# Attention and gated feed-forward on one core: a twelve-step pipeline over four tiles, packed row sums, a token-major output projection and queries transposed by DMA

## The chip, the cores and the metric

The kernel runs on one core of a Trainium2 chip. The metric is the device time of one execution in microseconds (us), taken as the median of several executions.

Engine names in the profile: PE is TensorE's matmuls, PEld its weight loads, DVE is VectorE, ACT is ScalarE, POOL is GpSimd, SP is SyncE. "L221" is line 221 of the kernel whose profile is shown. A "bank" is one of the eight 128 x 512 fp32 buffers in PSUM that both kernels allot for PE's results. An "eviction" is the copy of a full bank out of PSUM by ACT or DVE.

## The reference, cut to what matters

```python
# B=4, N=12288 queries per batch, C=128; kv: 384 x 32 positions per batch; d_ff=1536
kv_pool = kv.reshape(B, H//4, 4, W//4, 4, C).mean(axis=(2, 4))   # 768 pooled keys per batch
k = v = kv_pool.reshape(B, -1, C) @ w_sr
s = (q @ k.transpose(0, 2, 1)) / sqrt(C)
a = exp(s - s.max(-1)) ; a /= a.sum(-1) + 1e-9
x = a @ v                                       # attention output, 49152 tokens x 128
out = (relu(x @ w_gate) * (x @ w_val)) @ w_out  # fp32, 49152 x 128
```

Both kernels leave the normalisation to the end: relu and the product are homogeneous, so dividing x by the row sum r divides the output by r squared. They need r (one number per token) only at the output.

## The kernel before

It takes 512 tokens at a time ("a tile", 96 in all). Per tile it computes six score chunks, exp on ACT, six value chunks, row sums, twelve value and twelve gate projections, the output projection, and a turn of the output to token-major. The loop staggers the stages by one tile:

```python
def stage_r(k):                       # row sums: 1 weight column, 6 x 512 columns
    r_ps = psum.tile([1, TSUP], FP32, tag="bank")
    for jc in range(NJC):
        nc.tensor.matmul(r_ps, ones_a, aT[:, jc, :], ...)
    nc.scalar.copy(r_row, r_ps)
...
def stage_moe2(k):                    # output projection, feature-major
    for fb in range(NFB):
        nc.tensor.matmul(oT_ps, wo16[:, fb, :], hT[:, fb, :], ...)   # 12 x 512 columns
    nc.vector.tensor_copy(oT, oT_ps)
def stage_out(k):                     # back to token-major on PE
    for s in range(NSUB):
        nc.tensor.matmul(o_ps[:, s, :], oT[:, s*128:(s+1)*128], ident, is_transpose=True, ...)
    # four tensor_scalar by 1/r^2, then the store
...
for k in range(NTOT + 2):
    stage_qk(k, jcg(0)); stage_out(k - 2)
    stage_moe1(k - 1, [0]); stage_moe1(k - 1, [1])     # value and gate projections
    ...                                                # the rest interleaved; stage_tq: PE transposes
    stage_r(k); stage_rcol(k - 1); stage_moe2(k - 1); stage_load(k + 2)
```

Queries are loaded as fp32 and transposed on PE (`stage_tq`, four fp32 transposes per tile and one DVE copy). The pooled keys are summed by sixteen accumulating DMA transfers per batch on POOL's queue.

The softmax here doesn't subtract the row's maximum and nothing guards it: scores larger than these inputs give would overflow.

Of the kernel before, what the change touches and what calls it, by code (L numbers as in the profile page):

```python
# [9 lines left out]
FP32 = mybir.dt.float32  # L10
# [6 lines left out]
def kernel(  # L17
# [9 lines left out]
):  # L27
    nc = tc.nc
# [4 lines left out]
    HP, WP = H // r, W // r  # L33
    J = HP * WP
    D_FF = moe_w_gate.shape[1]
    NFB = D_FF // 128
    TSUP = 512
    NSUB = TSUP // 128
    NST = N // TSUP
    NJC = J // 128  # L40
    ALPHA = 1.0 / float(J)
    qk_scale = 1.0 / math.sqrt(C)

    assert N % TSUP == 0 and J % 128 == 0 and C == 128 and D_FF % 128 == 0
    assert NFB == 12 and NJC % 2 == 0
    assert J == 128 * NJC

    NTOT = B * NST

    cpool = ctx.enter_context(tc.tile_pool(name="const", bufs=1))  # L50
    wpool = ctx.enter_context(tc.tile_pool(name="wts", bufs=1))
    kvpool = ctx.enter_context(tc.tile_pool(name="kvp", bufs=1))
    spool = ctx.enter_context(tc.tile_pool(name="work", bufs=2))
    psum = ctx.enter_context(tc.tile_pool(name="psum", bufs=8, space=bass.MemoryType.PSUM))

    ident = cpool.tile([128, 128], FP32)
    make_identity(nc, ident)
    ones_a = cpool.tile([128, 1], FP16)
    nc.gpsimd.memset(ones_a, ALPHA)

    w_sr_f32 = wpool.tile([128, C], FP32)
    nc.sync.dma_start(w_sr_f32, w_sr)
    wg16 = wpool.tile([128, D_FF], FP16)
    wv16 = wpool.tile([128, D_FF], FP16)
    wo16 = wpool.tile([128, NFB, 128], FP16)
    for w16, src in (
        (wg16, moe_w_gate),
        (wv16, moe_w_val),
        (wo16, moe_w_out.rearrange("(fb f) c -> f fb c", f=128)),
    ):  # L70
        wstage = kvpool.tile([128, D_FF], FP32, tag="wstage")
        nc.sync.dma_start(wstage, src)
        nc.vector.tensor_copy(w16.rearrange("p ... -> p (...)"), wstage)

    kT_all = wpool.tile([128, B, NJC, 128], FP16)
    v_all = wpool.tile([128, B, NJC, 128], FP16)

    kv_tiles = {}

    def prep_dma(b):  # L80
        parts = []
        for dh in range(r):
            kvp = kvpool.tile([128, NJC, C], FP32, tag=f"kvp{dh}")
            first = True
            for dw in range(r):
                nc.gpsimd.dma_start(  # L86
                    kvp, kv[b][dh::r, dw::r, :],
                    accum_op=(ALU.bypass if first else ALU.add),
                )
                first = False  # L90
            parts.append(kvp)
        kv_tiles[b] = parts

    def prep_compute(b):
        parts = kv_tiles.pop(b)
        kvpT = kvpool.tile([128, NJC, C], FP32, tag="kvpT")
        for jc in range(NJC):
            tp_ps = psum.tile([128, 128], FP32, tag="bank")
            for dh in range(r):
                nc.tensor.matmul(  # L100
                    tp_ps, parts[dh][:, jc, :], ident, is_transpose=True,
                    start=(dh == 0), stop=(dh == r - 1),
                )
            nc.scalar.copy(kvpT[:, jc, :], tp_ps)
        for jc in range(NJC):
            kT_ps = psum.tile([128, 128], FP32, tag="bank")
            nc.tensor.matmul(kT_ps, w_sr_f32, kvpT[:, jc, :], start=True, stop=True)
            nc.scalar.mul(kT_all[:, b, jc, :], kT_ps, qk_scale / (r * r))  # L108
            v_ps = psum.tile([128, 128], FP32, tag="bank")
            nc.tensor.matmul(v_ps, kvpT[:, jc, :], w_sr_f32, start=True, stop=True)  # L110
            nc.scalar.mul(v_all[:, b, jc, :], v_ps, 1.0 / (r * r))

    prep_dma_at = {max(0, b * NST - 6): b for b in range(1, B)}
    prep_compute_at = {max(0, b * NST - 2): b for b in range(1, B)}

    qT_tiles = {}
    aT_tiles = {}
    xT_tiles = {}
    inv2_tiles = {}
    hT_tiles = {}  # L120
    val_tiles = {}
    rrow_tiles = {}
    qraw_tiles = {}

    def glob_tok(k):
        b = k // NST
        st = k % NST
        return b, b * N + st * TSUP, st * TSUP

    def stage_load(k):  # L130
        if not (0 <= k < NTOT):
            return
        b, _, n0 = glob_tok(k)
        q_raw = spool.tile([128, NSUB, C], FP32, tag="q_raw", bufs=4)
        nc.sync.dma_start(
            q_raw, q[b, n0 : n0 + TSUP, :].rearrange("(s p) c -> p s c", p=128)
        )
        qraw_tiles[k] = q_raw

    def stage_tq(k):  # L140
        if not (0 <= k < NTOT):
            return
        q_raw = qraw_tiles.pop(k)
        qT_ps = psum.tile([128, TSUP], FP32, tag="bank")
        for s in range(NSUB):
            nc.tensor.matmul(  # L146
                qT_ps[:, s * 128 : (s + 1) * 128], q_raw[:, s, :], ident,
                is_transpose=True, start=(s == 0), stop=(s == NSUB - 1),
            )
        qT = spool.tile([128, TSUP], FP16, tag="qT", bufs=3)  # L150
        nc.vector.tensor_copy(qT, qT_ps)  # L151
        qT_tiles[k] = qT

    def stage_qk(k, jc_list):
        if not (0 <= k < NTOT) or not jc_list:
            return
        b, _, _ = glob_tok(k)
        if jc_list[0] == 0:
            qT = qT_tiles[k]
            aT = spool.tile([128, NJC, TSUP], FP16, tag="aT", bufs=2)  # L160
            aT_tiles[k] = aT
        else:
            qT = qT_tiles[k]
            aT = aT_tiles[k]
        if jc_list[-1] == NJC - 1:
            qT_tiles.pop(k)
        for jc in jc_list:
            sT_ps = psum.tile([128, TSUP], FP32, tag="bank")
            nc.tensor.matmul(  # L169
                sT_ps, kT_all[:, b, jc, :], qT,  # L170
                start=True, stop=True,
            )
            nc.scalar.activation(aT[:, jc, :], sT_ps, AF.Exp)  # L173

    xtps_tiles = {}

    def stage_av(k, jc_list):
        if not (0 <= k < NTOT) or not jc_list:
            return
        b, _, _ = glob_tok(k)  # L180
        aT = aT_tiles[k]
        if jc_list[0] == 0:
            xt_ps = psum.tile([128, TSUP], FP32, tag="bank")
            xtps_tiles[k] = xt_ps
        else:
            xt_ps = xtps_tiles[k]
        for jc in jc_list:
            nc.tensor.matmul(  # L188
                xt_ps, v_all[:, b, jc, :], aT[:, jc, :],
                start=(jc == 0), stop=(jc == NJC - 1),  # L190
            )
        if jc_list[-1] == NJC - 1:
            xtps_tiles.pop(k)
            xT = spool.tile([128, TSUP], FP16, tag="xT", bufs=3)
            nc.vector.tensor_copy(xT, xt_ps)
            xT_tiles[k] = xT

    def stage_r(k):
        if not (0 <= k < NTOT):
            return  # L200
        aT = aT_tiles.pop(k)
        r_ps = psum.tile([1, TSUP], FP32, tag="bank")
        for jc in range(NJC):
            nc.tensor.matmul(  # L204
                r_ps, ones_a, aT[:, jc, :],
                start=(jc == 0), stop=(jc == NJC - 1),
            )
        r_row = spool.tile([1, TSUP], FP32, tag="r_row", bufs=2)
        nc.scalar.copy(r_row, r_ps)  # L209
        rrow_tiles[k] = r_row  # L210

    def stage_rcol(k):
        if not (0 <= k < NTOT):
            return
        r_row = rrow_tiles.pop(k)
        rcol_ps = psum.tile([128, NSUB], FP32, tag="bank")
        for s in range(NSUB):
            nc.tensor.matmul(  # L218
                rcol_ps[:, s : s + 1], r_row[0:1, s * 128 : (s + 1) * 128],
                ident[0:1, 0:1], is_transpose=True,  # L220
                start=(s == 0), stop=(s == NSUB - 1),  # L221
            )
        rinv = spool.tile([128, NSUB], FP32, tag="rinv", bufs=3)
        nc.vector.reciprocal(rinv, rcol_ps)
        tmp = spool.tile([128, NSUB], FP32, tag="rtmp", bufs=3)
        nc.vector.tensor_scalar(tmp, rinv, ALPHA, None, op0=ALU.mult)
        inv2 = spool.tile([128, NSUB], FP32, tag="inv2", bufs=4)
        nc.vector.tensor_tensor(inv2, tmp, tmp, op=ALU.mult)
        inv2_tiles[k] = inv2

    def stage_moe1(k, fb_list):
        if not (0 <= k < NTOT) or not fb_list:
            return
        if fb_list[0] == 0:
            hT = spool.tile([128, NFB, TSUP], FP16, tag="hT", bufs=2)
            val_sb = spool.tile([128, NFB, TSUP], FP16, tag="val_sb", bufs=2)
# [131 lines left out]
```

## Time and profile before

| | before |
|---|---|
| median of 3 runs | 1434.69 us (1434.51 to 1435.2) |
| profiled span | 1432.5 us |
| first loop matmul | about 61 us |
| one tile in the loop | 14.06 us |

The prediction below shows the totals, the timeline and the waits. Three groups of the page are worth adding, because the change rewrites them. Columns: line, engine, operation, output <- inputs, shape, count | busy us, mean ns of one | idle us of the engine just before, and what ended most of it.

```profile
L276 DVE COPY oT<-oT_ps 128x512 f32<-128x512 f32 x96 | 66.4, 692 | 173.4 <-PE oT_ps L271 173.4
L287 PE MATMUL o_ps<-ident,oT 128*128 128x128 f32 x384 | 62.8, 286 | 33.9 <-DVE oT L276 33.9
L204 PE MATMUL r_ps<-aT,ones_a 128*1 128x512 f16 x576 | 140.1, 378 | 0.0
```

The first two rows are one chain: DVE idles until the last output matmul, copies, and PE idles until the copy is there. The third row is 576 matmuls that use one of PE's 128 columns. Their "mean ns of one" (378) is the length of a pipelined matmul, not its cost; the cost is the distance between starts, 216 ns.

### The profile page before, as it was taken

How to read it: one execution, taken by the hardware profiler on the slowest of the kernel's cores; microseconds unless marked ns; L12 is line 12 of the kernel's file. 1: busy time of each engine (PE TensorE's matmuls, PEld its weight loads, DVE VectorE, ACT ScalarE, POOL GpSimd, SP SyncE). 2: the span in 40 equal slices, each digit the busy share in tenths (PEclk: the TensorE clock that was granted, in tenths of full speed). 3: DMA queues.
4: the chain of work that ended last, by engine and by line, in shares of the span. 5: the costliest groups of instructions: out<-in, count | busy, mean ns of one | idle time of the engine just before them, and what ended most of it. 6: DMA issues, size and time to landing. Idle time of an engine off the chain costs nothing.

```text
span 1432.5 us, 18941 instructions
## 1 busy us (share of the span) xinstructions
PE 1333.7 (93%) x6528; PEld 612.5 (43%) x6528; DVE 1039.6 (73%) x2115; ACT 947.7 (66%) x1897; POOL 81.7 (6%) x71
## 2 busy tenths in 40 slices
PE   0599999999999999999999999999999999999998
PEld 0344444444544444444454444444454444444443
DVE  0177777878677778787768787877767878777776
ACT  0367676767676767676667676766776766667674
POOL 5510000000220000000041000000000000000000
PEclk9999999999999999999999999999999999999999
DMA  9951111111591111111194111111111111111000
GB/s 229 179 93 38 37 45 30 45 30 45 101 148 32 45 30 44 32 43 37 38 169 81 30 45 35 40 37 37 39 36 31 45 37 38 37 37 40 28 23 23
DMA packets 142880, 79.14 MB, mean 55 GB/s; under 512 B 4160, under 2 KB 140992, under 8 KB 142784
## 3 DMA queue, kind: packets, MB, share of 16 engines
q1 hardware_dynamic: 103360, 52.77, 13.0%
q0 software_dynamic: 39424, 25.17, 12.0%
q8 instruction: 51, 0.84, 0.2%
q14 instruction: 45, 0.37, 0.1%
HBM read 52.76 MB, written 25.17 MB: 54 GB/s over the span
## 4 chain that ended last, share of the span: by engine, by line
PE 69%; ACT 21%; DVE 5%; DMA 3%; issue 1%; POOL 1%; DVEq 0%; POOLq 0%
PE oT_ps L271 18%; ACT val_sb L252 14%; PE g_ps L254 12%; PE va_ps L248 10%; PE r_ps L204 9%; PE xt_ps L188 9%; ACT aT L173 7%; DVE oT L276 5%; PE o_ps L287 4%; PE qT_ps L146 3%; DMA kvp<-in_kv_dram 3%; PE rcol_ps L218 2%; PE tp_ps L100 1%; POOL kvp L86 1%; ACT kT_all L108 0%
## 5 line engine op out<-in xcount | busy, mean ns | idle before, releaser
L258 DVE SCALAR_TENSOR_TENSOR hT<-g_ps,val_sb 128x512 f16<-128x512 f32 x1152 | 721.4, 682 | 48.0 <-PE va_ps L248 45.0
L252 ACT CAST val_sb<-va_ps 128x512 f16<-128x512 f32 x1152 | 611.4, 639 | 73.0 <-PE va_ps L248 73.0
L173 ACT ACTIVATE aT<-sT_ps 128x512 f16<-128x512 f32 x576 | 320.9, 625 | 239.1 <-PE sT_ps L169 239.1
L254 PE MATMUL g_ps<-xT,wg 128*128 128x512 f16 x1152 | 436.1, 379 | 9.7
L248 PE MATMUL va_ps<-xT,wv 128*128 128x512 f16 x1152 | 436.6, 379 | 0.1
L271 PE MATMUL oT_ps<-hT,wo 128*128 128x512 f16 x1152 | 265.3, 380 | 0.0
L276 DVE COPY oT<-oT_ps 128x512 f32<-128x512 f32 x96 | 66.4, 692 | 173.4 <-PE oT_ps L271 173.4
L169 PE MATMUL sT_ps<-qT,kT_all 128*128 128x512 f16 x576 | 171.0, 379 | 0.8 <-DVE qT L151 0.8
L293 DVE TENSOR_SCALAR o_sb<-o_ps,inv 128x128 f32<-128x128 f32 x384 | 108.1, 344 | 86.3 <-PE o_ps L287 86.3
L254 PEld LDWEIGHTS <-wg 128*128 128x128 f16 x1152 | 112.7, 98 | 116.8 <-issue 2.4
L248 PEld LDWEIGHTS <-wv 128*128 128x128 f16 x1152 | 112.6, 98 | 114.5 <-issue 1.3
L188 PE MATMUL xt_ps<-aT,v_all 128*128 128x512 f16 x576 | 155.9, 378 | 0.0
L271 PEld LDWEIGHTS <-wo 128*128 128x128 f16 x1152 | 104.8, 98 | 114.8
L204 PE MATMUL r_ps<-aT,ones_a 128*1 128x512 f16 x576 | 140.1, 378 | 0.0
L209 ACT COPY r_row<-r_ps 1x512 f32<-1x512 f32 x96 | 55.2, 575 | 98.3 <-PE r_ps L204 97.0
L86 POOL DMA_DIRECT2D kvp<-in_kv_dram x64 | 80.9, 1379 | 685.1 <-PE tp_ps L100 588.1
L151 DVE CAST qT<-qT_ps 128x512 f16<-128x512 f32 x96 | 66.4, 692 | 55.6 <-PE qT_ps L146 51.7
L287 PE MATMUL o_ps<-ident,oT 128*128 128x128 f32 x384 | 62.8, 286 | 33.9 <-DVE oT L276 33.9
L188 PEld LDWEIGHTS <-v_all 128*128 128x128 f16 x576 | 55.7, 97 | 77.0 <-issue 20.6
L169 PEld LDWEIGHTS <-kT_all 128*128 128x128 f16 x576 | 56.2, 98 | 68.6 <-DVE qT L151 1.0
L204 PEld LDWEIGHTS <-ones_a 128*1 128x1 f16 x576 | 40.2, 82 | 91.8 <-issue 41.3
L287 PEld LDWEIGHTS o_ps<-ident,oT 128*128 128x128 f32 x384 | 40.5, 140 | 80.2 <-DVE oT L276 76.9
(28 smaller groups left out, 374.9 us busy)
## 6 DMA issues: line engine op xcount, KB each, us to landing
kvp<-in_kv_dram POOLq DMA_DIRECT2D x64, 384.0 KB, 6.6
q_raw<-in_q_dram SPq DMA_DIRECT2D x96, 256.0 KB, 2.8
out_dram<-o_sb SPq DMA_DIRECT2D x96, 256.0 KB, 2.3
wstage<-in_moe_w_gate_dram SPq DMA_DIRECT2D x1, 768.0 KB, 4.5
wstage<-in_moe_w_val_dram SPq DMA_DIRECT2D x1, 768.0 KB, 5.8
wstage<-in_moe_w_out_dram SPq DMA_DIRECT2D x1, 768.0 KB, 6.4
w_sr_f<-in_w_sr_dram SPq DMA_DIRECT2D x1, 64.0 KB, 1.7
```

Of the source, the lines that this page charges most:

```text
L169: nc.tensor.matmul(sT_ps, kT_all[:, b, jc, :], qT, start=True, stop=True,)
L173: nc.scalar.activation(aT[:, jc, :], sT_ps, AF.Exp)
L188: nc.tensor.matmul(xt_ps, v_all[:, b, jc, :], aT[:, jc, :], start=(jc == 0), stop=(jc == NJC - 1),)
L204: nc.tensor.matmul(r_ps, ones_a, aT[:, jc, :], start=(jc == 0), stop=(jc == NJC - 1),)
L248: nc.tensor.matmul(va_ps, wv16[:, fb * 128 : (fb + 1) * 128], xT, start=True, stop=True,)
L252: nc.scalar.copy(val_sb[:, fb, :], va_ps)
L254: nc.tensor.matmul(g_ps, wg16[:, fb * 128 : (fb + 1) * 128], xT, start=True, stop=True,)
L258: nc.vector.scalar_tensor_tensor(hT[:, fb, :], g_ps, 0.0, val_sb[:, fb, :], op0=ALU.max, op1=ALU.mult,)
L271: nc.tensor.matmul(oT_ps, wo16[:, fb, :], hT[:, fb, :], start=(fb == 0), stop=(fb == NFB - 1),)
L276: nc.vector.tensor_copy(oT, oT_ps)
L287: nc.tensor.matmul(o_ps[:, s, :], oT[:, s * 128 : (s + 1) * 128], ident, is_transpose=True, start=(s == 0), stop=(s == NSUB - 1),)
L293: nc.vector.tensor_scalar(o_sb[:, s, :], o_ps[:, s, :], inv2[:, s : s + 1], None, op0=ALU.mult,)
```

## The change

Its intent: let PE never wait for the engine it has just fed, and take from PE what another unit can do or what uses it badly.

```diff
-    q_raw fp32; 4 PE transposes + DVE copy per tile
+    nc.gpsimd.dma_start(q16, q[...])                    # fp32 -> fp16 in the transfer, 4 tiles at once
+    nc.sync.dma_start_transpose(qT, q16...)             # 24 in all
-    nc.tensor.matmul(r_ps, ones_a, aT[:, jc, :])        # per tile, [1, 512]
+    for jc in range(NJC):                               # once per 4 tiles
+        for i in range(GRP):
+            nc.tensor.matmul(r_ps[32*i : 32*i+32, :], ones, aTs[g*GRP+i][:, jc, :])   # ones [128, 32]
-    nc.tensor.matmul(oT_ps, wo16[:, fb, :], hT[:, fb, :])              # 12 x 512, copy, 4 transposes
+    for s in range(NS):                                                # 48 x 128, token-major at once
+        nc.tensor.matmul(o_ps[:, s, :], hTs[k][:, fb, s*128:(s+1)*128], wo16[:, fb, :])
-    for k in range(NTOT + 2): stages of tile k, k-1, k-2 ...
+    for k in range(LAG, last + 1):                      # LAG = 3
+        for step in range(NFB):                         # twelve equal steps
+            out_proj(k - LAG - 1, step)
+            value_proj(k - LAG, step)
+            scores(k, step//2)  or  values(k - 1, step//2)
+            gate_proj(k - LAG, step)
+            # row sums in step 2, their transposes in step 5 of every fourth tile
-    kv pooled by accumulating DMA
+    kv loaded plainly (kv_in, 3 buffers, sync and ACT queues), added on DVE;
+    later batches loaded by the sync queue, added on POOL, projected inside the loop
```

The six key chunks of the first batch and the scores and values of the first four tiles run ahead of the loop.

## The prediction

> **What bounds the kernel now.** I read the busy totals first, then the chain of work that ended last, then sixteen microseconds of the timeline in mid-kernel, then the list of waits.
>
> ```profile
> PE 1333.7 (93%) x6528; PEld 612.5 (43%) x6528; DVE 1039.6 (73%) x2115; ACT 947.7 (66%) x1897; POOL 81.7 (6%) x71
> PE 69%; ACT 21%; DVE 5%; DMA 3%; issue 1%; POOL 1%; DVEq 0%; POOLq 0%
> ```
>
> TensorE (PE) is at work for 93% of the span and holds 69% of the chain; no other engine passes 73%. Matmuls overlap, so 93% isn't yet proof. The timeline of one loop turn gives the real paces (start, length, group, count):
>
> ```profile
> 700.34 0.40 PE L218 MATMUL rcol_ps<-ident,r_row 1*128 1x1 f32 x4
> ...
> 700.67 2.76 PE L271 MATMUL oT_ps<-hT,wo 128*128 128x512 f16 x12
> ...
> 704.22 0.66 PE L287 MATMUL o_ps<-ident,oT 128*128 128x128 f32 x4 [0.35 <-DVE oT L276]
> ...
> 708.97 3.12 ACT L252 CAST val_sb<-va_ps 128x512 f16<-128x512 f32 x6
> ...
> 709.75 3.67 DVE L258 SCALAR_TENSOR_TENSOR hT<-g_ps,val_sb 128x512 f16<-128x512 f32 x6
> ...
> 713.01 1.46 PE L204 MATMUL r_ps<-aT,ones_a 128*1 128x512 f16 x6
> ...
> 714.40 0.40 PE L218 MATMUL rcol_ps<-ident,r_row 1*128 1x1 f32 x4
> ```
>
> The same group returns after 714.40-700.34 = **14.06 us**: one 512-token tile. Twelve 512-column matmuls take 2.76 us, one alone 0.38, so the pace is (2.76-0.38)/11 = **0.216 us**. The row sums (one weight column) keep the same pace: (1.46-0.38)/5 = 0.216. Four fp32 transposes run at (0.66-0.286)/3 = 0.125 (0.11 where the queue is full). ScalarE (ACT) evicts one bank per 3.12/6 = **0.52**, VectorE (DVE) one per 3.67/6 = **0.61**.
>
> A tile has 54 matmuls of 512 columns (6 scores, 6 values, 6 row sums, 12 value, 12 gate, 12 output): 54 x 0.216 = 11.66. Eight fp32 transposes (queries, output) add 0.95, four row-sum transposes (0.40-0.20)/3 = 0.067 each, 0.27. Sum 12.9 of 14.06; the remaining 1.2 us is PE waiting. The waits say where (total us, times, longest):
>
> ```profile
> PEld o_ps L287 <- DVE oT L276: 76.9, 91, 0.8
> PEld qT_ps L146 <- DVE hT L258: 57.8, 94, 0.6
> PEld rcol_ps L218 <- issue: 41.6, 95, 0.4
> PEld L204 <- issue: 41.3, 98, 0.6
> ```
>
> Some 0.8, 0.6, 0.4 and 0.4 us per tile on the weight loader (part of each is covered by matmuls in flight): output projection, copy, transpose one after another; a transpose waiting for a bank; and two waits for nothing, each where the row sums begin or end.
>
> The start is the other piece, in the chain in order of time:
>
> ```profile
> 47.46 6.71 DMA kvp<-in_kv_dram
> 54.22 1.54 PE tp_ps L100 x6
> 61.05 1.47 PE sT_ps L169 x6
> ```
>
> Nothing useful runs on PE until 61 us: sixteen accumulating transfers come one by one. 61 + 96 x 14.06 + the tail is the 1432.5 us span.
>
> **What the Trainium skill says.** (1) "TensorE: Matmul & The Clock Gate", section "Back-to-back issue gap", gives about 56 ns as the isolated gap of a 128-column matmul but about 81 ns for a sustained stream of load-and-multiply pairs, and 131 ns for N=512. The trace disagrees with the last (0.216), so I trust the 81 only in part. (2) The same page, "Measured speedup vs the span model": three 32-column strips at once ran 2.38 times as fast as one after another. No strip runs beside another in the kernel before. (3) "TensorEngine Tiling (Array Packing)", section "Key Properties": changing the tiling mode drains the array. The two 0.4 us "issue" waits around the row sums agree with a drain. (4) "Advanced Engine Details and Errata", section "X-Bar Transpose (TRN2)", expects DMA transposes at 350-400 GB/s; no row before shows one.
>
> **The change, part by part**, per tile on PE:
>
> - Scores, values, value and gate projection stay: 36 x 0.216 = **7.78**.
> - Output projection is turned: hT becomes the stationary operand, so 12 matmuls of 512 columns (2.59) become 48 of 128 columns, each with its own weight load, and oT, its copy, four fp32 transposes and four small DVE scalings go. Columns are equal; the open term is the pair's pace. 512 columns in 0.216 scales to 0.054 plus overhead. Loads of 128x128 fp16 weights last 98 ns in the record, against 140 for fp32 and 82 for one column, so filling 128 fp16 columns seems to cost about 16 ns and should hide. I take 0.060: 48 x 0.060 = **2.88**. At 0.081 it would be 3.89.
> - Row sums of four tiles go to four 32-partition strips of one bank. If four stream at once: 6 x 0.216 = 1.30, plus two drains of 0.1, per four tiles: **0.38** per tile instead of 1.30. The row turns into a column by four fp32 transposes per four tiles: 4 x 0.11/4 = **0.11** instead of 0.27.
> - Query transposes leave PE (about 0.45) for 24 DMA transposes of 512 KB, and their DVE copy goes.
> - Sum: 7.78+2.88+0.38+0.11 = **11.15 us**.
>
> ACT has 12+6 evictions: 18 x 0.52 = 9.4; its row copy is gone. DVE has 12 products and one xT copy at 0.61, one output scaling of a whole bank at about 0.7 (estimated from the 0.69 copies) and a quarter of a row-sum copy and two small operations (0.24): 8.9 us. Both lie beside PE, so PE stays the bound, with less spare than the totals before suggest.
>
> The three-tile lag removes the chains: what PE multiplies in a step was made a step, or a tile, earlier. I keep **3%** of waits, because eight banks, two held for a whole tile by open sums, leave six in rotation with ACT at 84% and DVE at 80% of PE's period.
>
> The start: the keys now load plainly on two queues, are pooled on DVE, and four tiles of scores and values run while they arrive. 6.3 MB at the 203 GB/s which the kernel before moved in its first 72 us is 31 us; with queries and latency about 45 us until the loop, of which PE's 10 us of scores are part of the tile sums: 38 net. Pooling of later batches goes to POOL, idle so far, with slack of two tiles. Their 12 projections cost PE about 0.5 us each: 6. The tail: 6.
>
> Total: 96 x 11.15 = 1070; x 0.03 = 32; 38 + 6 + 6 = 50. **1152 us**, ratio 0.80.
>
> **Rivals.**
>
> A. The 128-column pairs are weight-bound. For: 81 ns in the skill, and over half of PE's matmuls come to be of this kind. Against: fp16 loads are short. It adds 48 x 0.021 x 96 = 97 us: about 1250.
>
> B. The strips don't run together (each strip's load waits for the multiply before). For: the drains. Against: the skill's 2.38. Row sums stay at 1.3 per tile: +0.92 x 96 = 88 us, about 1240.
>
> C. Evictions become the bound: DVE's end-of-tile burst (output scaling 0.7, xT 0.6) lets banks run out, so PE stalls about 1 us per tile: 1152 + 96 - 32, about 1215. It would show as PE waiting on DVE or ACT at value and gate projections.
>
> D. In-order queues. The built order puts 60 key loads into the sync queue ahead of the first output store, each fourth waiting for POOL to free a buffer; transposes wait there too. A slow POOL would hold back stores, then DVE and PE, early on: +20 to 40 us once. The DMA transposes are hidden anyway: one per 45 us, 1.5 us at the skill's rate; even ten times slower they fit.
>
> **Range and chances.** The floor is 0.056 per pair, no waits, a quick start: about 1100. One rival in part gives 1200-1240; two in full 1330, still under the 1406 which 2% needs. So 1105 to 1235; faster 0.95, same 0.03, slower 0.02.
>
> **What would show it.** Right: a four-tile period of 44.6-46 us; 48 output matmuls per tile at 0.056-0.065 spacing; row sums 24 in about 1.5 us; PE over 95% busy and no single wait above some 30 us in total; first loop matmul near 45 us. Wrong: spacing near 0.08 (A); row sums taking 5 us per group (B); PE waits on DVE or ACT near 1 us per tile (C); a hole of tens of us before the first stores (D). The prediction fails as a whole only if a DMA transpose takes over 45 us, or POOL starves the later batches.

## The result, and the profile after

| | before | after |
|---|---|---|
| median | 1434.6 us (4 runs) | 1127.94 us (4 runs, 1127.68 to 1128.06) |
| ratio | 1 | 0.7862, 95% interval 0.7851 to 0.7873 |
| profiled span | 1432.5 | 1125.7 |
| one tile in the loop | 14.06 | 43.75/4 = 10.94 |

The totals and the chain of the changed kernel, from its page:

```profile
PE 1077.6 (96%) x8874; PEld 636.3 (57%) x8874; DVE 920.1 (82%) x1470; ACT 909.2 (81%) x1741; POOL 119.8 (11%) x124
PE 94%; DMA 3%; ACT 1%; SPq 1%; DVE 0%; issue 0%; ACTq 0%; DVEq 0%; POOLq 0%
```

PE's share of the chain went from 69% to 94% and ACT's from 21% to 1%: the chain now runs from one matmul to the next. DVE and ACT carry more per unit of time than before and still aren't on it.

One and a half steps and a row-sum group in the timeline (start, length, group, count; other engines and the other matmuls of the steps are left out):

```profile
561.41 0.39 PE L221 MATMUL bank_ps<-wo,hT 128*128 128x128 f16 x4
...
562.28 0.39 PE L221 MATMUL bank_ps<-wo,hT 128*128 128x128 f16 x4
...
562.93 0.38 PE L207 MATMUL bank_ps<-xT,wg 128*128 128x512 f16 x1
563.24 0.98 PEld L170 LDWEIGHTS <-ones 128*32 128x32 f16 x24 [0.42 <-issue]
563.24 1.48 PE L170 MATMUL bank_ps<-aT,ones 128*32 128x512 f16 x24
...
564.65 0.40 PE L221 MATMUL bank_ps<-wo,hT 128*128 128x128 f16 x4
```

A step is 562.28 - 561.41 = 0.87 us: three 512-column matmuls at 0.216 and four 128-column ones at 0.056. That is what PE needs and nothing more. The 24 row-sum matmuls of four tiles start within 1.10 us; with the switch of PE to 32-column strips and back (0.31 us from the matmul before, 0.31 to the one after, where 0.216 is usual) they cost 564.65 - 562.93 - 0.216 = 1.50 us. Before, one tile's six cost 1.48 by the same count.

The waits of the changed kernel (total us, times, longest):

```profile
ACT val L200 <- PE bank_ps L196: 164.6, 568, 2.5
DVE hT L210 <- ACT val L200: 83.2, 312, 0.3
ACT L131 <- DMA parts<-in_kv_dram: 36.1, 1, 36.1
PE bank_ps L133 <- ACT kvT L131: 24.0, 2, 23.6
PE bank_ps L156 <- DVE o_sb L229: 2.1, 1, 2.1
```

ACT waits for PE and DVE for ACT, which is as it should be. Of the two waits of PE, one is at the start and one near 112 us. The start of the changed kernel, from the timeline:

```profile
0.74 35.30 ACTq L101 DMA_DIRECT2D parts<-in_kv_dram  x12
...
16.34 8.27 SPq L84 DMA_TRANSPOSE qT<-q  x1
...
36.07 1.28 ACT L131 ACT_TABLE_LOAD   x1 [36.07 <-DMA parts<-in_kv_dram]
```

ACT issues twelve key loads, and with three buffers the later ones wait until a buffer is free: its first work of its own comes at 36 us. Only then can PE project a key chunk (37.68 us); six chunks follow, some 3.9 us each, and the loop's first matmul is at 61.55 us, no earlier than before.

### The profile page after: what moved, and what is told of

The parts are those of the page before. It is cut to its first block, busy times and chain, and to the rows that moved or that the text cites. A ratio compares the mean times of both kernels' runs of the same rounds, so it can differ in the third digit from the quotient of the medians.

```text
span 1125.7 us, 23319 instructions
## 1 busy us (share of the span) xinstructions
PE 1077.6 (96%) x8874; PEld 636.3 (57%) x8874; DVE 920.1 (82%) x1470; ACT 909.2 (81%) x1741; POOL 119.8 (11%) x124
## 4 chain that ended last, share of the span: by engine, by line
PE 94%; DMA 3%; ACT 1%; SPq 1%; DVE 0%; issue 0%; ACTq 0%; DVEq 0%; POOLq 0%
PE bank_ps L221 23%; PE bank_ps L196 22%; PE bank_ps L207 22%; PE bank_ps L150 11%; PE bank_ps L156 11%; PE bank_ps L170 3%; DMA q<-in_q_dram 1%; PE bank_ps L133 1%; PE bank_ps L182 1%; DMA parts<-in_kv_dram 1%; SPq L84 1%; DMA out_dram<-o_sb 1%; ACT aT L151 1%; PE bank_ps L134 1%; PE bank_ps L126 0%
## 5 line engine op out<-in xcount | busy, mean ns | idle before, releaser
L210 DVE SCALAR_TENSOR_TENSOR hT<-bank_ps,val 128x512 f16<-128x512 f32 x1152 | 764.7, 687 | 133.4 <-ACT val L200 83.2
L200 ACT CAST val<-bank_ps 128x512 f16<-128x512 f32 x1152 | 676.5, 589 | 166.1 <-PE bank_ps L196 164.6
L221 PEld LDWEIGHTS <-hT 128*128 128x128 f16 x4608 | 349.7, 98 | 262.9 <-issue 10.2
L221 PE MATMUL bank_ps<-wo,hT 128*128 128x128 f16 x4608 | 441.1, 219 | 0.9 <-DVE hT L210 0.8
L196 PE MATMUL bank_ps<-xT,wv 128*128 128x512 f16 x1152 | 436.6, 379 | 0.2
L207 PE MATMUL bank_ps<-xT,wg 128*128 128x512 f16 x1152 | 436.6, 379 | 0.0
L151 ACT ACTIVATE aT<-bank_ps 128x512 f16<-128x512 f32 x576 | 344.9, 602 | 3.1 <-PE bank_ps L150 3.1
L156 PE MATMUL bank_ps<-aT,kv 128*128 128x512 f16 x576 | 216.6, 379 | 2.8 <-DVE o_sb L229 2.1
L150 PE MATMUL bank_ps<-qT,kv 128*128 128x512 f16 x576 | 216.3, 381 | 2.4 <-ACT kv L138 2.4
L150 PEld LDWEIGHTS <-kv 128*128 128x128 f16 x576 | 56.0, 98 | 6.2 <-ACT kv L138 4.0
L156 PEld LDWEIGHTS <-kv 128*128 128x128 f16 x576 | 56.3, 98 | 4.5 <-issue 1.2
L170 PE MATMUL bank_ps<-aT,ones 128*32 128x512 f16 x576 | 35.5, 381 | 0.0
```

The source lines that it names most:

```text
L150: nc.tensor.matmul(s_ps, kv16[:, k // NST, jc, 0, :], qT_of(k), start=True, stop=True)
L151: nc.scalar.activation(aTs[k][:, jc, :], s_ps, AF.Exp, scale=qk_scale)
L156: nc.tensor.matmul(xt_banks[k], kv16[:, k // NST, jc, 1, :], aTs[k][:, jc, :], start=(jc == 0), stop=(jc == NJC - 1),)
L170: nc.tensor.matmul(r_ps[32 * i : 32 * i + 32, :], ones, aTs[g * GRP + i][:, jc, :], start=(jc == 0), stop=(jc == NJC - 1),)
L196: nc.tensor.matmul(va_ps, wv16[:, fb * 128 : (fb + 1) * 128], xTs[k], start=True, stop=True)
L200: nc.scalar.copy(val, va_ps)
```

## The experiments

Eleven kernels were run against the kernel before, three rounds each; all gave correct results. The theory: PE is the bound throughout the loop, so each part is worth its PE time and the parts add; beyond that only the start is left. Rivals: a part is hidden or gives its gain back to another wait; evictions or banks are near their limit; the start is bound by the rate of transfers.

Unless said otherwise, each edit is against the changed kernel, and a loss or gain is the distance from its 1127.94 us. The changed kernel's stall of 2.4 us near 112 us (see s7) is in none of the traces of e1 to e6, which takes about 2 us off each of their losses.

### e1: the strips one after another in the program

A strip is 32 partitions of the row-sum bank, one strip for each of four tiles.

```diff
-        for jc in range(NJC):
-            for i in range(GRP):
+        for i in range(GRP):
+            for jc in range(NJC):
```

> The changed kernel with the two row-sum loops swapped: the six matmuls of one strip come one after another, then the next strip's. Same instructions, same results. Theory (strips of different tiles stream at once only when they follow each other directly; PE has no spare time to hide work in): the group of 24 takes about 24 x 0.216 = 5.2 us instead of 1.4, so +3.6 to +3.8 us per four tiles, +86 to +91 us in all, about 1215 us. Rival (the gain lies in the pipeline, the row sums hide in waits): 1128 us, unchanged.

Measured: 1158.36 us (1156.63 to 1160.04), ratio 0.8072 [0.8058, 0.8086]. The four-tile period is 45.08 us, 1.33 more than the changed kernel's 43.75. The loss is real but a third of what the theory said. The row-sum group in this kernel's timeline:

```profile
575.93 2.81 PE L170 MATMUL bank_ps<-aT,ones 128*32 128x512 f16 x24
```

All 24 starts lie within 2.43 us. One after another at 0.216 they would need 23 x 0.216 = 4.97 (which e6 measures). So strips still ran side by side, although the built program has six matmuls of one strip, then six of the next: starts of 216 ns spacing interleave with others 5 to 17 ns behind. The records don't name the strip, so which matmul passed which is inferred; the total isn't. This run undoes only part of the packing, and e6 replaced it.

### e6: all row sums in one strip

```diff
-        r_ps = bank([128, T])
-        for jc in range(NJC):
-            for i in range(GRP):
-                nc.tensor.matmul(r_ps[32*i : 32*i+32, :], ones, aTs[g*GRP+i][:, jc, :], ...)
+        for i in range(GRP):
+            r_ps = bank([128, T])
+            for jc in range(NJC):
+                nc.tensor.matmul(r_ps[0:32, :], ones, aTs[g*GRP+i][:, jc, :], ...)
+            nc.vector.tensor_copy(r_sb[32*i : 32*i+32, :], r_ps[0:32, :])
```

> The changed kernel with all row sums in the strip of partitions 0 to 31, one bank per tile, four VectorE copies of 32 partitions in place of one of 128. The swapped loops cost only 1.33 us per four tiles, because matmuls of two strips still ran side by side. Theory: one strip cannot overlap itself, so the 24 take 24 x 0.216 = 5.2 us, +3.8 us per four tiles, +91 us: about 1219 us. Rival (the 1.41 us come from small weights or the short drain, not from strips side by side): 1128 to 1160 us.

Measured: 1219.05 us (1218.49 to 1220.88), ratio 0.8501 [0.8488, 0.8514]; period 47.63. The 24 starts now span 4.97 us, exactly 23 x 0.216, against 1.10 in the changed kernel, and the period grew by the same 3.88. So the bank per tile and the four copies, which also changed, cost nothing. Running four strips together is worth 1219.05 - 1127.94 = 91 us. From its page, the group's busy time, where overlap counts once (35.5 in the changed kernel):

```profile
L171 PE MATMUL bank_ps<-aT,ones 128*32 128x512 f16 x576 | 128.5, 379 | 0.0
```

### e3: the output projection as before

`out_proj` again multiplies 12 x 512 columns feature-major; a DVE copy and four fp32 transposes follow one tile later, so they stay out of PE's way.

```diff
-            nc.tensor.matmul(o_ps[:, s, :], hTs[k][:, fb, s*128:(s+1)*128], wo16[:, fb, :], ...)
+        nc.tensor.matmul(o_banks[k], wo16[:, fb, :], hTs[k][:, fb, :], ...)
+        # then, one tile later: copy to oT, 4 fp32 transposes, scaling, store
```

> The changed kernel with the output projection as it was before (wo16 stationary, 12 matmuls of 512 columns, copy, four fp32 transposes one tile later), all else as changed. Theory (PE-bound, each PE nanosecond counts): 12 x 0.2157 - 48 x 0.0559 + 4 x 0.109 = +0.34 us per tile, +33 us, about 1161. Rival (VectorE's extra copy of 0.6 us and one more bank make evictions the bound): +60 us or more. Other rival (the turned projection is worth nothing, its transposes were hidden): within 6 us of 1128.

Measured: 1157.41 us (1156.64 to 1158.55), ratio 0.8065 [0.8053, 0.8077]; period 45.14, so 1.39 us more. As expected: the four transposes cost 0.44 us per tile, and dropping the 48 pairs (a weight load and a 128-column matmul each) gives back 48 x 0.0559 - 12 x 0.216 = 0.09.

### e4: queries transposed on PE

```diff
-        nc.gpsimd.dma_start(q16, ...)                    # fp16
-        nc.sync.dma_start_transpose(qT, q16...)
+        nc.sync.dma_start(q32, ...)                      # fp32
+        # four fp32 PE transposes and one DVE copy per tile, in step 8
```

> The changed kernel with fp32 query loads on the sync queue and four fp32 PE transposes plus a VectorE copy per tile, as before, in place of the DMA transposes. Theory: steady state +4 x 0.109 = 0.44 us per tile, +42 us; but at the start the sync queue no longer stands still for two transposes of 8 us, so 15 to 20 us come back: 1150 to 1155 us, with a four-tile period of 45.5 us against 43.75. Rival (the start is bound by transfer rate, not by the transposes in the queue): 1165 to 1172 us.

Measured: 1160.66 us (1159.25 to 1161.26), ratio 0.8085 [0.8073, 0.8097]; period 45.50, 1.75 more, which is 16 x 0.109. The loop is as expected; the start gained about 3 us (loop at 58.8) where the theory hoped for 15 to 20, so the total lies between theory and rival. Only 22 of the 24 groups are transposed inside the loop, which makes 38 us there and not 42. In the changed kernel's trace the DMA transposes are hidden: 24 of them, a median of 4.3 us from issue to landing, one per 44 us.

### e5: e1, e3 and e4 together

> The changed kernel's loop, lag, buffers and start, but with all three PE savings given back: output projection and its transposes as before, queries transposed by PE, row-sum loops swapped. Theory (parts add, because PE never waits in this loop): the single runs gave +29.5, +32.7 and +30.4 us, so 1128 + 93 = 1221 us, a four-tile period of about 43.75 + 1.39 + 1.75 + 1.33 = 48.2 us with no PE wait; what is left to the kernel before (about 214 us) is the pipeline, the strips that overlap even so, and the start. Rival (the extra copies load VectorE, so waits come back): 1245 us or more.

Measured: 1222.13 us (1221.1 to 1223.76), ratio 0.8521 [0.8509, 0.8534]; period 48.22. The three alone cost 30.4 + 29.5 + 32.7 = 92.6 us over 1127.94; together they cost 94.2. The periods add exactly: 1.33 + 1.39 + 1.75 = 4.47, and 48.22 - 43.75 = 4.47. That is what a single saturated engine looks like.

### e2: the output matmuls in one block

```diff
-            if 0 <= kO:
-                out_proj(kO, step)
...
+            if 0 <= kO and step == NFB - 1:
+                for fb in range(NFB):
+                    out_proj(kO, fb)
```

> The changed kernel with the 48 output matmuls of a tile in one block in its last step instead of four in each of twelve steps. PE does the same work. Theory (the spreading feeds ScalarE and VectorE evenly): for 2.7 us per tile they get nothing, and in the other steps PE runs at 0.65 us per step against 0.8 us that ScalarE needs, so PE waits for banks: +0.3 to +0.7 us per tile, 1157 to 1195 us. Rival (six free banks absorb it, the order within a tile is of no account): within 6 us of 1128.

Measured: 1152.67 us (1151.16 to 1157.09), ratio 0.8036 [0.8018, 0.8054]; period 44.67, 0.92 more, just below the expected range. The amount of PE work is the same; only its order changed. Without the output matmuls a step is 0.65 us of PE work, while one eviction lasts about 0.6 us on ACT and every second step has an exp besides, so PE can outrun ACT until the block of output matmuls lets it catch up. In this kernel's trace the 0.92 us lie in small lengthenings of the distance between starts: 0.51 in all before the 24 score matmuls of four tiles, 0.30 before value projections, 0.12 after scores, where the changed kernel has 0.216 everywhere. The matmuls that come late each need a free bank, but the profile marks most of these waits as issue, so that the bank is what they wait for is argued, not shown. Evenly spread output matmuls are worth 25 us.

### s1: six key buffers instead of three

```diff
-        parts = work.tile([128, r, r, C], FP32, tag="kv_in", bufs=3)
+        parts = work.tile([128, r, r, C], FP32, tag="kv_in", bufs=6)
```

> The changed kernel with six key buffers instead of three. At the start ScalarE's queue holds 12 key loads ahead of its first copy, and the last of them wait for VectorE to free a buffer, which waits for loads behind the first query transpose in the sync queue. Theory (buffers tie the queues together): ScalarE's first copy comes at about 25 us instead of 37, 8 to 12 us gained: 1116 to 1120 us. Rival (the start is bound by the transfer rate and by the transpose in the sync queue): within 4 us of 1128.

Measured: 1127.71 us (1124.54 to 1130.36), ratio 0.7861 [0.7845, 0.7877]: nothing gained. ACT was free at 21 us instead of 36, but a second wait took over, and then a third. The start in this kernel's timeline:

```profile
16.67 11.07 SPq L84 DMA_TRANSPOSE qT<-q  x1
...
35.18 1.87 PE L150 MATMUL bank_ps<-qT,kv 128*128 128x512 f16 x4 [11.53 <-DMA qT<-q]
```

The query transpose landed only at 35 us, so the loop began at 59.8. Those 2 us were lost near 115 us, where the stall of the changed kernel grew from 2.5 to 5.5 us between two matmul starts. (The profile is of the slowest of four runs, 1130.36 us.)

### s5: keys first, first queries on PE, copies on DVE

Six buffers; all first-batch key loads issued first; the first four tiles transposed by PE in fp16; projection copies on DVE rather than ACT.

```diff
-    q_turn(0)
+    for jc in range(NJC): kv_load(0, jc, hw)
+    # 16 PE transposes of q16 against an fp16 identity, copies on DVE
-        project(0, jc, s1, nc.scalar.copy, act_scaled)
+        project(0, jc, s1, nc.vector.tensor_copy, dve_scaled)
```

> As the run with six key buffers, and all first-batch key loads queued first, the first four query tiles transposed by PE in fp16, and the copies of the first batch's projection on VectorE so that ScalarE does only exponentials. Theory: PE starts near 16 us, a key chunk takes some 2.5 us instead of 3.9, and the loop begins where the keys have landed, 40 to 46 us instead of 61.5: 1108 to 1114 us. Rival (transfer rate: 6.3 MB of keys share the queues with 1 to 4 MB of queries and the weights): loop at 50 to 55 us, 1117 to 1122.

Measured: 1124.22 us (1123.32 to 1124.82), ratio 0.7838 [0.7825, 0.7851]. The loop began at 51.6 us, 10 earlier, yet only 3.7 us reached the end. The rest was lost at 109 us. DVE, then the sync queue, of this kernel:

```profile
108.71 0.69 DVE L229 TENSOR_TENSOR o_sb<-bank_ps,inv 128x512 f32<-128x512 f32 x1 [7.67 <-DMA out_dram<-o_sb]
```

```profile
89.64 10.66 SPq L101 DMA_DIRECT2D parts<-in_kv_dram  x10
100.91 0.42 SPq L232 DMA_DIRECT2D out_dram<-o_sb  x1
102.03 9.86 SPq L101 DMA_DIRECT2D parts<-in_kv_dram  x11
```

DVE has the next output ready to scale but no free output buffer. The store of the first tile, scaled by 70.5 us, was issued behind key loads of the next batch (the last ten are in the line above it), at 100.91 us, and landed only when DVE's wait ended, 7.8 us later, where such a store takes 2.2 (median of the changed kernel). The wait reaches PE as a gap of 7.5 us. More buffers allow more prefetched loads, which is why s1 made it worse too.

### s7: the changed kernel, with later batches' key loads on POOL's queue

```diff
-                    kv_load(b, at, [nc.sync])
+                    kv_load(b, at, [nc.gpsimd])
```

> The changed kernel with only the key loads of the later batches moved to POOL's queue. Theory (stores stuck behind key loads): the gap of 2.5 us before the values matmul at 112 to 114 us goes, the rest stays; median 1123 to 1126 us. Rival (the store is late for the transfer rate, or POOL's additions come late because POOL waits to issue loads): the gap stays or moves, median 1127 us or more.

Measured: 1125.48 us (1125.05 to 1127.2), ratio 0.7849 [0.7837, 0.786]. The first four-tile period fell from 44.76 to 42.34 us, so the 2.4-us stall is gone, and the rest is as it was. In both traces the first tile is scaled by about 81 us; its store was issued at 81.1 us here and at 105.4 in the changed kernel. The rival, slow transfers, does not fit: the stores issued here at 101.7 and 112.2 us took 9.7 and 10.3 us to land, longer than the 8.2 us of that store in the changed kernel, and nothing stalled. Stores held back by loads in one queue were its cause.

### s6: an early query load as well

Six buffers; the first query group loaded as fp32, half by each queue, ahead of the keys; transposed on PE; copies on DVE; later keys on POOL's queue.

> Six key buffers; the first four query tiles are loaded as fp32 by two queues ahead of the key loads and transposed by PE, the first-batch projection copies are on VectorE, and the key loads of the later batches are issued by POOL's queue. Theory (the start is a chain of the query load, a blocked queue and copies on ScalarE; the stall at 100 to 115 us is an output store stuck behind key loads in the same queue): the loop's first matmul at 40 to 46 us instead of 61.5, no gap over 2 us between 100 and 120 us, median 1108 to 1114 us. Rival (the rate at which inputs and first outputs move sets the start, whichever queue issues them): the loop begins after 52 us or a gap of over 3 us remains, median 1120 us or more.

Measured: 1113.04 us (1112.71 to 1115.62), ratio 0.7765 [0.7752, 0.7778]. No stall over 1 us remained between 50 and 1100 us, and the median is in the range of the theory, but the loop began at 49.5 us, between the two expectations. The timeline of its start shows why:

```profile
13.62 0.66 PE L126 MATMUL bank_ps<-ident,s 128*128 128x128 f32 x4 [1.88 <-DVE s L112]
...
22.53 0.69 DVE L110 TENSOR_TENSOR s<-parts 128x512 f32<-128x512 f32 x1 [1.40 <-DMA parts<-in_kv_dram]
23.14 0.68 DVE L261 CAST qT<-bank_ps 128x512 f16<-128x512 f32 x1
...
26.80 0.28 DVE L131 COPY kvT<-bank_ps 128x128 f32<-128x128 f32 x1
```

The first key chunk was transposed by about 14 us. Its copy came at 26.80, because DVE's built order puts the key additions of later chunks, each waiting for its transfer, ahead of it.

### s8: the start's copies on ACT, its key loads on one queue

The edit is against s6:

```diff
-        kv_load(0, jc, hw)
+        kv_load(0, jc, [nc.sync])
-        nc.vector.tensor_copy(qTs[0][...], qT_ps)
+        nc.scalar.copy(qTs[0][...], qT_ps)
-        project(0, jc, s1, nc.vector.tensor_copy, dve_scaled)
+        project(0, jc, s1, nc.scalar.copy, act_scaled)
```

> As the run before it with an early query load and later keys on POOL's queue, but all first-batch key loads are issued by the sync queue alone and every copy of the start (query casts, projection copies) is on ScalarE, which issues one load only. There the loop began at 49.5 us because VectorE took key additions, which waited for data, ahead of the query casts (key copy at 26.8 us although its transpose was done at 14). Theory (in-order VectorE held the start back, not the transfers): first projection at 14 to 16 us, six chunks of 3.9 us, loop at 39 to 43 us, median 1104 to 1108 us. Rival (one queue, or the rate of transfers, now sets the pace of the chunks): loop after 46 us, median 1110 us or more.

Measured: 1107.96 us (1107.08 to 1111.58), ratio 0.7723 [0.771, 0.7736]. The first projection came at 15.0 us, as the theory said, and the loop at 45.5, between theory and rival (the median is just inside the range of the theory). Both hold in turn: the copies no longer wait, and now DVE waits for key data, as in this line of its timeline:

```profile
23.19 0.69 DVE L110 TENSOR_TENSOR s<-parts 128x512 f32<-128x512 f32 x1 [3.00 <-DMA parts<-in_kv_dram]
```

A stall of 2.3 us at 105 us is in this run, which s6 had not. Its timeline:

```profile
102.81 3.71 DVE L191 TENSOR_TENSOR inv<-rinv 128x16 f32<-128x16 f32 x1
...
107.18 0.38 PE L196 MATMUL bank_ps<-xT,wv 128*128 128x512 f16 x1 [2.31 <-DVE hT L210]
```

PE waited for DVE, which spent 3.71 us on an instruction that takes 0.17 to 0.18 in its 23 other places in this trace. POOL's key additions ran all through it and paused as it ended (102.10 to 106.49 us), but in the changed kernel the same instruction took only 0.22 us beside two of POOL's additions, so what held it stays open. The profile is of the slowest of the four runs (1111.58 us; the others took 1107.08 to 1108.26), so they may not have this stall. s8 beats both kernels: 20 us less than the changed one.

## Why the prediction was right

The time fell inside the predicted range, 24 us below the point. The mechanism held, PE as the bound and a sum of its work per tile. Two of the prediction's own signs of being right did not: the four-tile period is 43.75 us, below its 44.6 to 46, and the loop's first matmul came at 61.5 us, not near 45. By its steps:

**The sum per tile** held: 11.15 predicted, 10.94 measured. Scores, values and projections cost 7.77 as said, the row sums 1.50 us per four tiles as said, the row-sum transposes 0.11. The pair pace was taken at 0.060 and is 0.0559: 48 x 0.0041 x 96 = 19 us too much.

**The 3% of waits** (32 us) never came. Outside the start and one stall, PE waits for almost nothing. The step "leave six in rotation" was over-cautious as long as the steps are even; e2 shows that waits do come, 25 us of them, when they aren't.

**The start** was sized too small. "About 45 us until the loop" came to 61.5. The prediction counted bytes over a rate, but the start was a chain: loads waiting for buffers in ACT's queue, then a query transpose behind them, then copies. s1, s5, s6 and s8 took these waits away one by one, and each time the next one appeared. Net of the 10.4 us of scores and values that count in the tile sums, the start is 51 us where 38 was written (and 45 - 10 would have been 35): +13.

**The later key projections** were put at 12 times 0.5 us. There are 18 (three batches of six chunks), and one costs 0.82: in the two four-tile periods of each batch change, 47.03 and 45.39, the excess over 43.75 is 4.92 us. That makes 15 us where 6 was written: +9. The trace before had the size: at each of its three batch changes a turn takes 18.9 us instead of 14.06, 14.5 us in all, which the reading "61 + 96 x 14.06 + the tail" left in the tail.

**The rivals.** A (pairs bound by weight loads) is refuted by 55.9 ns in the trace and by e3. B (strips not together) is refuted by e6, where it would have stood. C (evictions and banks) showed, if anywhere, only in e2. D came true, small: 2.4 us in the changed kernel where 20 to 40 was feared, 5.5 and 7.5 in s1 and s5; s7 shows its cause (58 key loads stand before the first store in the sync queue of the trace, where 60 was written). The DMA transposes are hidden in the loop, as said, though one takes 4.3 us from issue to landing where 1.5 was estimated; at the start they are not hidden.

The balance is 1152 - 19 - 32 + 13 + 9 + 2 = 1125, against a span of 1125.7. Two large errors, waits too many and a start too short, partly cancelled: that the total came within 24 us is in part luck.

**Where the 307 us came from.** One tile fell by 3.12 us. Row sums: 1.48 became 0.375, so 1.11. Query transposes: 0.44 (e4). Output projection with its transposes: 0.35 (e3). Row-sum transposes: 0.16 (0.27 became 0.11). What is left, 3.12 - 2.06 = 1.06 us, is waiting that the pipeline removed. No experiment measured this last term alone, but the trace before holds it: beyond the usual distance between starts, a tile waits 0.52 us before the output transposes, 0.35 between value and gate matmuls and 0.15 around the fp32 transposes, 1.02 in all, and in the changed kernel's loop these are gone. The prediction's 1.2 us included 0.19 at the row sums, which is charged to them here; the waits between value and gate matmuls it didn't name. Times 96 the five give 300 us; the remaining 7 lie outside these sums and aren't split further.

## What to carry to other kernels

When one engine is the bound, add up its work per period at the spacing of starts, and distrust allowances for waits where each step feeds every engine its even share. Then read the start as a chain, not as bytes over a rate: each in-order queue or engine that is made to wait for a buffer or a transfer holds back everything behind it, including stores and copies that have nothing to do with it. Removing one such wait shows little until the next is gone: six buffers alone gave nothing, while with the further changes of s8 the kernel became 20 us faster.

## What the Trainium skill lacked or had wrong

- "TensorE: Matmul & The Clock Gate", "Back-to-back issue gap", gives 81 ns (N=128) and 131 ns (N=512) for a sustained stream of load-and-multiply pairs. In the loop of the changed kernel, with a weight load for every matmul, starts are 55.9 ns and 215.8 ns apart: the figures that the page calls isolated hold for the stream.
- The same page, "The mechanism", says that matmuls start and end in strict program order. e1's 24 matmuls, six per strip in a row, started within 2.43 us where that order allows no less than about 4.3 us (an estimate: 20 steps at 0.216, since only the last of one strip and the first of the next could start together). Which matmul overtook which isn't in the records.
- The same page, "Measured speedup vs the span model", has three column strips at 2.38 times and four row strips at 3.07, and no figure for four column strips. Here four took 1.50 us with both mode switches, one strip alone (e6) 5.38 by the same count: 3.6 times.
- "TensorEngine Tiling (Array Packing)", "Key Properties", says that a mode change drains the array but not what it costs. Here it was 0.09 us each way (a distance of 0.31 where 0.216 is usual).
- "Advanced Engine Details and Errata", "X-Bar Transpose (TRN2)", says that transposes are as fast as other DMAs. Over the whole run a transpose of 512 KB landed 4.3 us after its issue (median), a store of 256 KB after 2.2, which agrees. But at the start, among key loads, the issue alone held its queue for 8.3 us (11.1 in s1), and in the loop for some 1.8. The section doesn't warn of that.
